# Shift gradient's rounds five job pieces sooner, and the last row block of w1's gradient summed in two column halves

## The chip, the core and the metric

The kernel runs on one core of one Trainium2 chip. The metric is the device time of one execution in microseconds (us). Before the change it is 702.48 us, the median of 3 runs (701.94 to 702.93).

A core has engines that work side by side, each with its own instruction queue, executed in order: TensorE (PE, matrix products; its weight loads are shown apart as PEld), VectorE (DVE), ScalarE (ACT), GpSimd (POOL) and SyncE (SP). SP, ACT and POOL also issue DMA transfers, each from its own queue. Engines wait for one another with semaphores. Matrix products are written to PSUM, a small memory of banks, and ACT or DVE copy them from there.

## The reference

The reference runs a four-layer model forwards, and then computes the gradients of its output with respect to eight inputs. S = 2048 rows, D = 448 columns, F = 1792 hidden columns, all in bf16.

```
x = A_q
x = x + A(layernorm(x), k, v, shift_k, ssm_k, ssm_D)   # A: k_shift = 4-tap causal shift of k weighted by shift_k
x = x + B(layernorm(x), w1, w2)                         #    kv = k_shift * v
x = x + A(layernorm(x), ...)                            #    y  = causal convolution of kv with ssm_k over S (FFT) + kv * ssm_D
x = x + B(layernorm(x), w1, w2)                         #    A  = q * y          (q is the normed x)
return x                                                # B: silu(x @ w1) @ w2
outputs: x, and the gradients for A_q, k, v, shift_k, ssm_k, ssm_D, w1, w2
```

Two of the outputs matter here. Output 7 is the gradient of w1, a 448 x 1792 matrix: the sum, over both B layers, of (normed input of the layer)ᵀ times (gradient at the hidden layer). Output 4 is the gradient of shift_k, a 448 x 4 matrix: for each of the 448 channels and each of the four taps, the sum over all 2048 rows of k, shifted, times the gradient of k_shift.

## The kernel before, in words

The kernel has a prefix (FFT of the convolution's kernel and of kv), a main part (the four layers forwards and backwards, in four chunks of 512 rows) and a suffix (`_ssm_suffix`: the gradients that go backwards through the FFT, and those of k, v, shift_k, ssm_k and ssm_D).

**Job pieces.** The weight gradients of w1 and w2 are long sums that need nothing but operands which the main part has stored in DRAM. The class `Jobs` holds them as a generator (`steps`): each step, a *piece*, puts four matmuls on PE. The suffix calls `jobs.run(n)` between its own steps, and each such call puts n pieces into PE's instruction order at that place. `jobs.run(1000)` on the last line of the suffix takes what is left. PE's order is exactly this written order (`manual_schedule`); the instructions of the other engines are put in order by the framework's scheduler.

**One row block of w1's gradient.** The gradient is computed transposed, in 14 row blocks of 128 of the 1792 hidden columns. For a block, `group` loads two stationary operands from DRAM (`dstat`, 128 x 2048 each, one for each layer, on SP's queue), and `mms` sums 2 x 16 matmuls into one PSUM bank (`ps_d`, 128 x 448, line L1046): 16 with the moving operand `n3m`, 16 with `n1m`. These are eight pieces. `fin_w1` then copies the sum with ACT to SBUF (`dout`, L1120), and `flush` does the rest for the block *before*: four transposes on PE (`ps_dt`, L1133), a copy to `wts` (L116 on ACT), and a DMA to output 7 (L1136). That block's flush so lies behind the sum of the block after it. For blocks 0 to 11 the DMA is issued by POOL, for block 12 by SP and for block 13 by ACT; block 13's copy to `wts` is on DVE (L117). Banks for `ps_d` are taken in turn by `bank(None)` from the tags "po", "tr" and "po", each of two buffers.

**The shift gradient.** After the last products of the ssm_k gradient (`ps_gK`, L1300), the suffix computes the shift gradient in four *rounds* r (`ps_sk`, L1322, two buffers of the tag "mm"): 64 small matmuls on 32 x 32 blocks of the array (32 in the last round), whose diagonals DVE reads out with a mask (`skjunk`, L1325). Before round 0 stands `jobs.run(8)`, after each round `jobs.run(3)`. Then DVE casts the result (`gskb`, L1329 and L1331), three further pairs of rows of the k gradient (`g_k`) are written on DVE and POOL, `jobs.run(3)` follows, and four matmuls with the identity turn the result (`ps_r`, L1337, in a buffer of the tag "po"). ACT copies it (`gsr`, L1339), and two DMAs store it, one on SP (L1341) and one on POOL (L1342). Last stands `jobs.run(1000)`.

With these numbers of pieces, the pieces of the last block end in the `jobs.run(3)` behind round 2, and `jobs.run(1000)` issues no matmul any more. L1370 is the closing code at the end of the program: each queue waits for its transfers and drains, then all engines meet.

Of the kernel before, what the change touches and what calls it, by code (L numbers as in the profile page):

```python
# [17 lines left out]
P = 128  # L18
S = 2048
D = 448  # L20
F = 1792
J = 16
NT = 16
DC = 112
ND = 4
# [88 lines left out]
def _copy(nc, eng, out, in_):  # L114
    if eng is nc.scalar:
        return nc.scalar.copy(out, in_)  # L116
    return eng.tensor_copy(out, in_)  # L117
# [18 lines left out]
def kernel(  # L136
# [63 lines left out]
    with tc.manual_schedule(engines={nc.tensor.engine}):  # L200
        with ExitStack() as es:
            Main(k, es).run(ys)
        _ssm_suffix(k)
# [369 lines left out]
class Main:  # L573
# [142 lines left out]
    def first_norm(self, xc, n00, n01):  # L716
        prs = ((0, 2), (2, 4))
        steps = [_ln_parts(self.k, self.ch, 0, self.xs(0), 1, n01, (pr,), True) for pr in prs]
        for pr, step in zip(prs, steps):
            self.gate(0, lambda tl: xc[:, tl, :], n00, (pr,), self.tc.keep_in_program_order)  # L720
            if pr[0]:
                next(steps[0], None)
            next(step)
        next(steps[1], None)
# [277 lines left out]
class Jobs:  # L1002
# [37 lines left out]
            nc.sync.dma_start_transpose(out=st, in_=src[ft, :, :])  # L1040
        return st

    def mms(self, ps, st, mov, lo, hi, first, last):
        for t0 in range(lo, hi, 4):
            for t in range(t0, t0 + 4):
                self.nc.tensor.matmul(ps[:, :D], lhsT=st[:, t, :], rhs=mov[:, t, :], start=(first and t == 0), stop=(last and t == NT - 1))  # L1046
            yield 1

    def bank(self, tag):
        if tag is None:  # L1050
            tag = ("po", "tr", "po")[self.n_bank % 3]
            self.n_bank += 1
        bufs = 2
        if tag == "mm":
            return self.k.psum.tile([P, 2, 512], FP32, name="ps_d", tag="mm", bufs=2)[:, 0, :]
        return self.k.psum.tile([P, 512], FP32, name="ps_d", tag=tag, bufs=bufs)[:]
# [25 lines left out]
    def steps(self):  # L1082
        g2 = lambda: self.k.mov2
        go = lambda: self.go
        keys = (("a", 1), ("a", 0))
        yield from self.group((0, 1, 2), keys, (go, g2), self.fin_w2, 12, ("tr", "po", "mm"))
        for f in range(3, 12):
            yield from self.group((f,), keys, (go, g2), self.fin_w2, tags=("tr",) if f == 3 else None)
        yield from self.group((12, 13), keys, (go, g2), self.fin_w2)
        keys = (("g", 1), ("g", 0))  # L1090
        movs = (lambda: self.n3, self.n1)
        yield from self.group((0, 1, 2), keys, movs, self.fin_w1)
        for f in range(3, 14):
            yield from self.group((f,), keys, movs, self.fin_w1)
        self.flush()

    def n1(self):
# [20 lines left out]
    def fin_w1(self, ft, ps):  # L1118
        o = self.out()
        self.nc.scalar.copy(o[:], ps[:, :D])  # L1120
        self.flush()
        self.pend = (ft, o)

    def flush(self):
        nc, k = self.nc, self.k
        if self.pend is None:
            return
        ft, o = self.pend
        self.pend = None
        out7v = k.outs[7].rearrange("(c p) f -> p c f", p=DC)  # L1130
        pt = k.psum.tile([DC, ND, P], BF16, name="ps_dt", tag="tr", bufs=2)
        for dc in range(ND):
            nc.tensor.transpose(pt[:, dc, :], o[:, dc * DC:(dc + 1) * DC], k.ident[:])  # L1133
        o7 = k.do7[ft % 4]
        _copy(nc, nc.vector if ft == 13 else nc.scalar, o7, pt[:])
        (nc.scalar if ft == 13 else nc.sync if ft == 12 else nc.gpsimd).dma_start(out=out7v[:, :, ft * P:(ft + 1) * P], in_=o7)  # L1136


def _s1_gy(k, rows):
# [6 lines left out]
def _ssm_suffix(k):  # L1146
    nc, tc, bal = k.nc, k.tc, k.bal
    jobs = k.jobs
# [6 lines left out]
    with ExitStack() as es:  # L1155
# [29 lines left out]
        for g in range(7):  # L1185
            pt = psum.tile([P, 2, 16, 64], BF16, name="ps_tr", **mm)
# [78 lines left out]
        for i in range(8):  # L1265
# [7 lines left out]
            last = nc.scalar.copy(gkv, py[:, :, :D])  # L1273
# [34 lines left out]
        gDr = sp.tile([ND, DC], BF16, name="gDr")  # L1308
        nc.scalar.copy(gDr[:], pr[:ND, :DC])
        nc.gpsimd.dma_start(out=k.outs[6].rearrange("(c p) -> c p", p=DC), in_=gDr[:])  # L1310
        jobs.run(8)
        mask = sp.tile([P, 32], BF16, name="mask")
        for q in range(4):
            nc.vector.tensor_copy(mask[32 * q:32 * q + 32, :], k.ident[32 * q:32 * q + 32, 32 * q:32 * q + 32])
# [60 lines left out]
```

## Time and profile before

| | before |
|---|---|
| median of the runs | 702.48 us (701.94 to 702.93) |
| profiled execution, its own time | 701.8 us |
| span of the profiled execution | 700.0 us |
| granted TensorE clock | 0.998 of full speed |
| DMA traffic over the span | 66.05 MB read, 54.60 MB written |

The profile comes from one execution. Its span runs from the first to the last instruction; the time of the execution is 1.8 us longer. Lines of the timeline read: start in us from the span's beginning, length in us, engine, line of the kernel, operation, what is written `<-` what is read, shapes, and xN where N instructions were merged; in brackets stands how long the engine had been idle and who released it. A "q" behind an engine's name is its queue, which issues DMAs and waits. The length of a merged run of matmuls holds the latency of its last one, so the pace of a run is read from two runs of different lengths, or from the start of one to the start of the next. The lines of the closing code give the count of instructions, their shortest, median and longest duration in ns, and the first and the last start. For DMAs the profile gives the size and the time from issue to landing.

### The profile page before, as it was taken

The page shows a single profiled execution, that of the slowest core. Times are in us where ns is not written, and L with a number is a line of the kernel's source. Part 1 is how long each engine was busy: PE and PEld are TensorE (multiplying, and loading weights), DVE is VectorE, ACT ScalarE, POOL GpSimd, SP SyncE. Part 2 cuts the span into 40 slices and gives each one's busy share as a digit, 9 for nine tenths or more (in the row PEclk, how much of TensorE's full clock was granted, in tenths as well). Part 3 has the DMA queues.
Part 4 walks back from the last instruction along what each step waited for, and adds up shares of the span by engine and source line. Part 5 has one row for each costly group of instructions (what it writes and reads, how often), then busy time and mean ns, then how long its engine had stood idle before and what let it go on. Part 6 is the DMA issues. An engine that isn't in the chain of part 4 may idle for free.

```text
span 700.0 us, 14553 instructions
## 1 busy us (share of the span) xinstructions
PE 666.0 (95%) x5897; PEld 358.8 (51%) x5933; DVE 484.1 (69%) x1131; ACT 432.9 (62%) x522; POOL 101.3 (14%) x173
## 2 busy tenths in 40 slices
PE   6898789999999999999999999999999999999996
PEld 5876545454444444434444444544554555555664
DVE  6688862676889948899578874853946545538991
ACT  5888766968856857769577585223554553554431
POOL 1057110110011100111000100010111211102311
PEclk9999999999999999999999999999999999999999
DMA  8999938459899976698677799959557888966981
GB/s 321 270 298 306 376 84 210 118 107 243 219 231 249 246 200 166 146 240 221 185 165 194 194 242 329 262 172 229 177 208 280 307 279 307 352 188 215 331 293 42
DMA packets 199798, 161.03 MB, mean 230 GB/s; under 512 B 147698, under 2 KB 180213, under 8 KB 198963
## 3 DMA queue, kind: packets, MB, share of 16 engines
q1 hardware_dynamic: 184550, 111.78, 58.8%
q0 software_dynamic: 10368, 36.29, 15.3%
q10 hardware_dynamic: 4812, 12.04, 5.0%
q8 instruction: 46, 0.75, 0.4%
q14 instruction: 22, 0.17, 0.1%
HBM read 66.05 MB, written 54.60 MB: 172 GB/s over the span
## 4 chain that ended last, share of the span: by engine, by line
PE 57%; DVE 22%; issue 10%; ACT 5%; POOL 3%; DMA 2%; POOLq 0%; DVEq 0%; ACTq 0%
PE ps_d L1046 19%; PE ps_n L836 8%; PE ps_h L638 6%; PE ps_g L638 6%; PE ps_o L798 5%; DVE ln_st L301 2%; DVE lb_v L994 2%; PE ps_v L265 2%; PE ps_cv L449 2%; POOL rstd L306 2%; DVE n L309 1%; DVE lb_v L997 1%; DVE lb_v L998 1%; DVE X L802 1%; PE ps_h L642 1%
## 5 line engine op out<-in xcount | busy, mean ns | idle before, releaser
L1046 PEld LDWEIGHTS <-dstat 128*128 128x128 bf16 x896 | 84.0, 98 | 77.8 <-issue 4.0
L836 PE MATMUL ps_n<-w1T,ghT 128*128 128x448 bf16 x448 | 96.6, 353 | 2.0 <-DVE ghT L821 1.7
L798 PE MATMUL ps_o<-w2sb,aT 128*128 128x448 bf16 x448 | 89.2, 353 | 0.7 <-DVE X L802 0.7
L638 PE MATMUL ps_h<-nT,w1sb 128*128 128x512 bf16 (+1 forms) x410 | 83.5, 336 | 2.2 <-ACT Dall L116 1.0
L116 ACT CAST ghT<-ps_g 128x1024 bf16<-128x1024 f32 (+1 forms) x54 | 48.4, 899 | 58.4 <-PE ps_g L642 47.7
L638 PE MATMUL ps_g<-nT,w2T 128*128 128x512 bf16 x317 | 77.9, 379 | 2.2 <-DVE Dall L117 0.5
L836 PEld LDWEIGHTS <-ghT 128*128 128x128 bf16 x448 | 41.4, 98 | 50.7 <-DVE ghT L821 6.7
L798 PEld LDWEIGHTS <-aT 128*128 128x128 bf16 x448 | 43.2, 98 | 41.1 <-issue 2.8
L638 PEld LDWEIGHTS <-w1sb 128*128 128x128 bf16 x420 | 39.2, 98 | 36.7 <-issue 7.2
L781 ACT ACTIVATE aT<-ps_h 128x1024 bf16<-128x1024 f32 (+1 forms) x48 | 44.2, 921 | 19.4 <-PE ps_h L638 10.5
L116 ACT CAST Dall<-ps_h 128x1024 bf16<-128x1024 f32 (+2 forms) x60 | 54.3, 904 | 0.0
L994 DVE SCALAR_TENSOR_TENSOR lb_v<-lb_u,n 128x448 bf16<-128x448 bf16 x60 | 37.2, 620 | 24.6 <-ACT lb_u L840 24.1
L791 ACT ACTIVATE Dall<-Dall 128x1024 bf16<-128x1024 bf16 (+1 forms) x48 | 53.2, 1186 | 0.1
L638 PEld LDWEIGHTS <-w2T 128*128 128x128 bf16 x336 | 31.3, 98 | 42.1 <-issue 7.2
L306 POOL TENSOR_TENSOR rstd<-ln_ve,mhalf 128x2 f32<-128x2 f32 (+1 forms) x24 | 19.9, 831 | 221.1 <-DVE ln_ve L305 221.1
L1046 PE MATMUL ps_d<-X,dstat 128*128 128x448 bf16 x224 | 47.9, 353 | 0.0
L1046 PE MATMUL ps_d<-go,dstat 128*128 128x448 bf16 x224 | 47.2, 353 | 0.0
L1046 PE MATMUL ps_d<-n3m,dstat 128*128 128x448 bf16 x224 | 46.4, 353 | 0.0
L1046 PE MATMUL ps_d<-n1m,dstat 128*128 128x448 bf16 x224 | 46.3, 353 | 0.0
L840 ACT ACTIVATE lb_u<-ps_n,rstd 128x448 bf16<-128x448 f32 x32 | 20.5, 640 | 28.7 <-PE ps_n L836 24.3
L116 ACT CAST A1g<-ps_v 128x1024 bf16<-128x1024 f32 x14 | 14.9, 1066 | 36.5 <-PE ps_v L265 36.5
L802 DVE TENSOR_TENSOR X<-X,ps_o 128x448 bf16<-128x448 bf16 x32 | 19.5, 610 | 21.3 <-PE ps_o L798 21.1
(206 smaller groups left out, 1111.6 us busy)
## 6 DMA issues: line engine op xcount, KB each, us to landing
dstat<-a_d SPq DMA_DIRECT2D x28, 512.0 KB, 5.0
dstat<-g_d SPq DMA_DIRECT2D x28, 512.0 KB, 5.2
a_d<-turned SPq DMA_DIRECT2D x16, 512.0 KB, 3.0
g_d<-turned SPq DMA_DIRECT2D x16, 512.0 KB, 3.2
a_d<-turned SPq DMA_DIRECT2D x16, 384.0 KB, 2.7
g_d<-turned SPq DMA_DIRECT2D x16, 384.0 KB, 3.0
spec_K<-KAB POOLq DMA_DIRECT2D x7, 512.0 KB, 5.4
KAB<-KAB POOLq DMA_DIRECT2D x28, 128.0 KB, 4.6
```

The lines of the kernel that those rows point to most:

```text
L116: return nc.scalar.copy(out, in_)
L265: nc.tensor.matmul(pv[:, r ^ (ci & 1), i, :], lhsT=src[ri, i * P:(i + 1) * P], rhs=k.Gsb[ri, g, ri], start=first, stop=not first)
L306: nc.gpsimd.tensor_tensor(out=r[:, lo:hi], in0=ve[:, lo:hi], in1=k.mhalf[:, lo:hi], op=ALU.pow)
L638: self.nc.tensor.matmul(ps, lhsT=w[:, b, ft * P:(ft + 1) * P], rhs=x[:, b], start=(start and b == 0), stop=(stop and b == bs[2]))
L781: self.last_silu = nc.scalar.activation(aT[hh][:, o:o + hi - lo, :], ps(lo, hi), ACT.Silu)
L791: self.nc.scalar.activation(dT[hh][:, o:o + n, :], dT[hh][:, o:o + n, :], ACT.Derivative_silu)
L798: nc.tensor.matmul(po[:, :D], lhsT=aT[ft // 7][:, ft % 7, tl * P:(tl + 1) * P], rhs=self.w2sb[:, ft, :], start=(ft == 0), stop=(ft == NF - 1))
L802: self.last_o = nc.vector.tensor_tensor(out=X[:, t, :], in0=X[:, t, :], in1=po[:, :D], op=ALU.add)
L836: nc.tensor.matmul(pn[:, :D], lhsT=gh[ft // 7][:, ft % 7, tl * P:(tl + 1) * P], rhs=self.w1T[:, ft, :], start=(ft == 0), stop=(ft == NF - 1))
L840: nc.scalar.activation(u0[:], pn[:, :D], ACT.Identity, scale=k.rstd[2 * L + 1][:, t:t + 1], accum_out=cp[:, tl, 0:1])
L994: nc.vector.scalar_tensor_tensor(out=v[:], in0=u0, scalar=-1.0 / D, in1=n_t, op0=ALU.mult, op1=ALU.mult, accum_out=cp[:, 1:2])
L1046: self.nc.tensor.matmul(ps[:, :D], lhsT=st[:, t, :], rhs=mov[:, t, :], start=(first and t == 0), stop=(last and t == NT - 1))
```

## The change

First, `jobs.run(8)` before the shift gradient's rounds becomes `jobs.run(3)`. Five pieces (20 matmuls) that stood before round 0 come behind it, and everything after it in PE's order moves with respect to the pieces.

Second, block 13 of w1's gradient is no longer made by `group` but by a new function, `last`. It loads both stationary operands and sums the two halves of 224 columns one after the other, each in a bank of its own and with all 32 stationary operands: 64 matmuls of 224 columns in place of 32 of 448. ACT copies each half (two copies of 224 columns). `flush` takes the range of transposes that it is to do: block 12 is flushed in half 0 behind its seventh piece, half 0 in half 1 behind its third piece, half 1 at the end.

Third, block 13's two stores are issued by SP (two halves, each behind a DVE copy of 256 columns), and block 12's store by POOL.

In PE's order of the changed kernel, the first rounds stand behind 8 matmuls of block 12 (n3m), 12 more, and 12 more; the fourth stands behind the first 12 narrow matmuls of block 13. `ps_r` stands behind the first 4 narrow matmuls of half 1, and waits for ACT, whose copy of half 0 frees its bank. Behind it follow 8 narrow matmuls, two transposes of half 0, 20 narrow matmuls, and two transposes of half 1. SP's last transfers are the shift gradient's and then the two halves' stores; POOL's last are the stores of blocks 10, 11 and 12 and the shift gradient's. DVE's order is the same but for the copies of `ps_dt` at its end. Lines behind L1048 are 17 or 18 higher in the changed kernel (L1133 is L1151, L1337 is L1355, L1370 is L1388); ACT's copy of a half is L1061.

```diff
-    def mms(self, ps, st, mov, lo, hi, first, last):
+    def mms(self, ps, st, mov, lo, hi, first, last, cols=slice(0, D)):
         for t0 in range(lo, hi, 4):
             for t in range(t0, t0 + 4):
-                self.nc.tensor.matmul(ps[:, :D], lhsT=st[:, t, :], rhs=mov[:, t, :], start=(first and t == 0), stop=(last and t == NT - 1))
+                self.nc.tensor.matmul(ps[:, cols], lhsT=st[:, t, :], rhs=mov[:, t, cols], start=(first and t == 0), stop=(last and t == NT - 1))
             yield 1
+
+    def last(self, ft, keys, movs):
+        nc, k = self.nc, self.k
+        sts = [self.load(key, ft) for key in keys]
+        o = self.out()
+        for h in range(2):
+            cols = slice(h * D // 2, (h + 1) * D // 2)
+            ps = self.bank(None)
+            for i in range(2):
+                for n, _ in enumerate(self.mms(ps, sts[i], movs[i](), 0, NT, i == 0, i == 1, cols)):
+                    if h + i == 1 and n == 2:
+                        self.flush()
+                    yield 1
+            nc.scalar.copy(o[:, cols], ps[:, cols])
+            if h == 0:
+                self.flush()
+            self.pend = (ft, o, 2 * h, 2 * h + 2)
...
-        for f in range(3, 14):
+        for f in range(3, 13):
             yield from self.group((f,), keys, movs, self.fin_w1)
+        yield from self.last(13, keys, movs)
         self.flush()
...
-        self.pend = (ft, o)
+        self.pend = (ft, o, 0, ND)
...
-        ft, o = self.pend
+        ft, o, lo, hi = self.pend
...
-        for dc in range(ND):
+        for dc in range(lo, hi):
             nc.tensor.transpose(pt[:, dc, :], o[:, dc * DC:(dc + 1) * DC], k.ident[:])
         o7 = k.do7[ft % 4]
-        _copy(nc, nc.vector if ft == 13 else nc.scalar, o7, pt[:])
-        (nc.scalar if ft == 13 else nc.sync if ft == 12 else nc.gpsimd).dma_start(out=out7v[:, :, ft * P:(ft + 1) * P], in_=o7)
+        _copy(nc, nc.vector if ft == 13 else nc.scalar, o7[:, lo:hi], pt[:, lo:hi])
+        (nc.sync if ft == 13 else nc.gpsimd).dma_start(out=out7v[:, lo:hi, ft * P:(ft + 1) * P], in_=o7[:, lo:hi])
...
         nc.gpsimd.dma_start(out=k.outs[6].rearrange("(c p) -> c p", p=DC), in_=gDr[:])
-        jobs.run(8)
+        jobs.run(3)
         mask = sp.tile([P, 32], BF16, name="mask")
```

## The prediction

> **What bounds the kernel now.** I read the page's busy rows first, then the end of the chain of waits, then the timeline of the last 25 us, and last the closing instructions.
>
> ```profile
> PE 666.0 (95%) x5897; PEld 358.8 (51%) x5933; DVE 484.1 (69%) x1131; ACT 432.9 (62%) x522; POOL 101.3 (14%) x173
> ```
> ```profile
> 686.23 9.93 issue
> 696.15 0.54 POOLq L1370
> ```
>
> TensorE (PE) is busy 95% of the span, so any matmul time added or any hole in its stream shows. The chain, however, ends not on PE but on POOL, which idles 9.93 us and then issues the last transfer. The timeline shows what POOL waited for:
>
> ```profile
> 690.22 2.44 PE L1046 MATMUL ps_d<-n1m,dstat 128*128 128x448 bf16 x12
> 692.59 1.07 PE L1322 MATMUL ps_sk<-kx_s,gks 128*32 128x128 bf16 x32
> 693.59 0.65 PE L1133 MATMUL ps_dt<-ident,dout 128*112 128x128 bf16 x8
> 694.06 0.59 ACT L116 COPY wts<-ps_dt 112x512 bf16<-112x512 bf16 x1 [0.83 <-PE ps_dt L1133]
> 694.34 0.42 DVE L117 COPY wts<-ps_dt 112x512 bf16<-112x512 bf16 x1
> 694.67 0.34 SPq L1136 DMA_DIRECT2D out_dram<-wts  x1
> 694.68 0.15 DVE L1331 CAST gskb<-gsk 64x4 bf16<-64x4 f32 x1
> 694.89 0.39 PE L1337 MATMUL ps_r<-ident,gskb 128*4 128x128 bf16 x4 [0.64 <-DVE gskb L1331]
> 695.31 0.57 ACT L1339 CAST gsr<-ps_r 4x512 bf16<-4x512 f32 x1 [0.66 <-PE ps_r L1337]
> 695.91 0.32 SPq L1341 DMA_DIRECT2D out_dram<-gsr  x1
> 696.17 0.52 POOL L1342 DMA_DIRECT2D out_dram<-gsr  x1 [9.95 <-ACT gsr L1339]
> ```
>
> PE has no hole to 694.2. The last shift-gradient round (ps_sk, 692.59) is followed by DVE's gskb, PE's ps_r and ACT's gsr; only then do SP (695.91) and POOL (696.17) issue the shift gradient's two stores. Two queues then close:
>
> ```profile
> L1370 SPq EVENT_SEMAPHORE  x2: 28/28/28, 697.3 to 697.9; - x2
> L1370 SPq DRAIN  x2: 7/7/7, 698.3 to 698.4; - x2
> L1370 POOLq DRAIN  x1: 3064/3064/3064, 696.2 to 696.2; - x1
> L1370 PEldq EVENT_SEMAPHORE  x1: 51/51/51, 700.0 to 700.0; - x1
> out_dram<-wts SPq DMA_DIRECT2D x1, 112.0 KB, 2.3
> SPq L1370 <- DMA out_dram<-gsr: 0.6, 1, 0.6
> ```
>
> SP sees its last store land at 697.9 (695.91 + 2.0) and is drained at 698.4. POOL's drain starts at 696.15 with its last issue and takes 3.06 us, to 699.2; 0.8 us of common closing follow. So POOL sets the end, 0.8 us after SP would.
>
> **The change part by part.** Quoted once, the steps of PE that both versions share, and the widths that the halves need:
>
> ```profile
> 676.83 3.19 PE L1046 MATMUL ps_d<-n3m,dstat 128*128 128x448 bf16 x16
> 682.22 1.08 PE L1322 MATMUL ps_sk<-kx_s,gks 128*32 128x128 bf16 x64
> 683.23 0.93 PE L1046 MATMUL ps_d<-n1m,dstat 128*128 128x448 bf16 x4
> 684.00 0.39 PE L1133 MATMUL ps_dt<-ident,dout 128*112 128x128 bf16 x4
> 684.22 1.68 PE L1046 MATMUL ps_d<-n3m,dstat 128*128 128x448 bf16 x8
> 685.83 1.08 PE L1322 MATMUL ps_sk<-kx_s,gks 128*32 128x128 bf16 x64
> 686.84 1.69 PE L1046 MATMUL ps_d<-n3m,dstat 128*128 128x448 bf16 x8
> 689.21 1.08 PE L1322 MATMUL ps_sk<-kx_s,gks 128*32 128x128 bf16 x64
> 30.49 0.94 PE L465 MATMUL ps_s<-ks_kv,M1sb 128*128 128x224 bf16 x8
> L465 PE MATMUL ps_s<-ks_kv,M1sb x64: 256/259/270, 30.5 to 52.4; 128*128 128x224 bf16 x64
> ```
>
> *Rounds five pieces sooner.* A piece is four matmuls; 20 of them move behind round 0. At (1.68 − 0.93)/4 = 0.19 us each (runs of 8 and of 4) that is 3.8 us: round 0 starts at 678.44 (676.83 + 1.61, the step from 684.22 to 685.83) instead of 682.22. Are its operands there? kx is, and DVE reads a round's result late:
>
> ```profile
> 652.02 1.41 ACTq L1285 DMA_DIRECT2D kx_s<-in_A_k_dram  x2
> DMA to landing us min/median/max: 13.7/13.9/14.2
> 681.29 1.09 DVE L1261 TENSOR_TENSOR gk<-wx 128x896 bf16<-128x896 f32 x1
> 683.35 0.19 DVE L1325 SCALAR_TENSOR_TENSOR skjunk<-ps_sk,mask 128x32 bf16<-128x32 f32 x1 [0.97 <-PE ps_sk L1322]
> ```
>
> kx landed by 667. DVE keeps its order, so round 0's four readings (at most 4 × 0.19 us) wait for gk, to 682.4, and are done by 683.2. The two banks of ps_sk make round 2 wait for that; it starts at 685.2. The cover is 2.0 us, and DVE's order puts nothing else before it; were it gone, PE would stand for what gk is later than that. Cost: nothing.
>
> *The halves.* 64 matmuls of 224 columns replace 32 of 448. L465 has this very form: (0.94 − 0.26)/7 = 0.097 us each, so 6.21 us for 32 × 0.19 = 6.08, **+0.13 us**. ACT gains one copy; block 12's store goes from SP to POOL (0.7 us of POOL, before it waits for gsr, so nobody waits for it).
>
> *PE's new schedule*, the generated order with the steps above: round 0 678.44 to 679.45; 12 matmuls (686.84 to 689.21 = 2.37), round 1 681.82 to 682.83; 12 (690.22 to 692.59 = 2.37), round 2 685.20 to 686.21; four transposes 0.22, to 686.43; 12 narrow 1.16 and 0.10 for the turn to a round (2.37 − 12 × 0.19, rounded), round 3 687.69 to 688.69 (692.59 to 693.59 = 1.00); 16 narrow 1.55, to 690.24; block 12's four transposes, 690.46; the last 4 narrow of half 0 and the first 4 of half 1, 691.24.
>
> *A new wait.* ps_r, next on PE, needs the bank that half 0 held, so it waits for ACT's copy of half 0. ACT comes to that late: its store copy of block 12 waits for the transposes (690.24 + 0.39), runs from 690.67, and the next ACT instruction starts 0.47 behind it (670.30 to 670.77 below), 691.14. A copy of 224 columns takes 0.53 less half the column cost, (1.01 − 0.53)/576 × 224 = 0.19, so 0.35: done 691.49, ps_r at 691.55. PE stands **0.31 us** in order; everything left of half 1 is queued behind it. Bounds: 0 (if ACT's start is 0.3 earlier) and 0.6 (copy at the full width's 0.53, and a delay of ACT of 0.1).
>
> ```profile
> 670.30 0.59 ACT L116 COPY wts<-ps_dt 112x512 bf16<-112x512 bf16 x1
> 670.77 0.21 ACT L1304 COPY gKD<-gK 112x1 bf16<-112x1 bf16 x1
> 672.02 1.01 ACT L1301 CAST gK<-ps_gK 112x1024 bf16<-112x1024 f32 x1 [1.04 <-PE ps_gK L1300]
> 692.70 0.53 ACT L1120 CAST dout<-ps_d 128x448 bf16<-128x448 f32 x1 [7.48 <-PE ps_d L1046]
> ```
>
> *The new tail.* ps_r 0.22, to 691.77; gsr on ACT and both its stores follow by 692.7, so POOL's drain ends near 692.9 + 3.0 = 695.9 and bounds nothing. PE goes on: 8 narrow 0.78, 2 transposes of half 0 0.11, 20 narrow 1.94, to 694.60; the last one's result 0.16 later, 694.76. ACT 0.04 + 0.35, 695.15. PE 0.05 + 0.28 (the four's 0.39 less two steps), 695.48. DVE 0.04 + 0.30 (half the columns of 0.42, whose ends are 0.21 and 0.42), 695.82. SP issues at **695.84**, just where its last store went before (695.91).
>
> Landing: the 3 KB gsr took 2.0 us, a whole block's store 2.3; half a block 2.15, between. So 697.99 (before 697.9). SP's remaining semaphores and drain took 697.9 to 698.4; 0.45 gives 698.44, bounds 0.1 (its semaphore is the last asked for) and 0.5. Closing as before, 0.8: the span ends at **699.24 for 700.0, −0.76 us**. The gain is POOL's late drain, nothing more: PE's stream gets longer, and the SP queue's last issue stays. The profiled execution took 701.8 (1.8 outside the span), the median is 702.48; I take the difference off the median: **701.7**.
>
> **A rule weighed.** The Trainium skill, "TensorE: Matmul & The Clock Gate", section on LDWEIGHTS, prices a weight load at its columns over 1.2, 107 ns for 128. If that paced the narrow matmuls, 64 × 0.010 = 0.64 us would come on top, an estimate from that page, and 702.4. The trace's L465 spacing of 97 ns disagrees with it as a pace.
>
> **The rivals.**
> - *Much of the tail is early* (faster): no stall at ps_r (−0.31), landing in 2.0 (−0.15), SP's semaphore last asked for (−0.35): 0.76 + 0.81 = 1.57, 700.9. For it: each is an end of a bound above. Against: all three are needed, since 1.4 us decides.
> - *POOL's drain follows the last landing, not POOL's own issue* (no gain): it ended 1.1 us behind the last store's landing (696.17 + 1.9 = 698.1). Then 697.99 + 1.1 + 0.8 = 699.9, 702.4. Against: it began with POOL's issue. That would be the change not doing what it says.
> - *Weight loads pace the narrow matmuls* (slower): one load takes 97 ns and half 1 loads all 32 stationaries again. Unhidden, a matmul would cost 0.097 twice, 64 × 0.097 = 6.2 us more, 708; it decides from 0.131 us a matmul (2.16 us more eats the gain and 1.4). Against: the 0.097 spacing holds while a load of 97 ns runs under each.
>
> ```profile
> L465 PEld LDWEIGHTS <-M1sb 128*128 128x128 bf16 x64 | 5.9, 97 | 2.1 <-issue 0.8 <-DVE ks_kv L455 0.3
> DMA to landing us min/median/max: 1.9/1.9/1.9
> ```
>
> **How the numbers follow.** 0.2% is 1.4 us, about what a measurement of this kernel can tell from no change. My forecast (a small gain inside that) 0.50 and the drain rival 0.12 make "same" 0.62; the early tail, with gains that I have not seen, 0.27 faster; the weight-load rival 0.06 and an unseen stall 0.05 slower. Range: down to the early tail's 700.9 with 0.3 for the runs' own scatter (701.94 to 702.93), 700.6; up to the drain rival's 702.4 with 0.5 for it, 702.9.
>
> **What would show it.** Right: four ps_sk groups from about 678.4, 681.8, 685.2 and 687.7; narrow ps_d matmuls 97 ns apart; ps_r near 691.5 with a hole of about 0.3 us before it that ACT's dout ended; SP's last store at 695.8; POOL's 3 us drain over by 696; the span near 699.2. Wrong: a narrow spacing above 0.13 us, a POOL drain that still ends after SP's, or a hole at round 2 or at the last transposes.

## The result and the profile after

The changed kernel takes 701.64 us (median of 19 runs, 700.62 to 702.49), the kernel before, measured beside it, 702.85 (19 runs, 701.82 to 703.62): ratio 0.9978, 95% interval 0.9971 to 0.9984, so 0.22% less (0.16 to 0.29). Run again later (e8 below, 12 runs, with 35 of the kernel before beside them), the ratio was 0.9987, interval 0.9975 to 0.9999. The kernel is faster, by 0.22% in one series and 0.13% in the other; both intervals end below 1. The profiled execution took 700.62, its span is 698.8 for 700.0.

First the page's busy line of the changed kernel, and from its chain of waits the last pieces:

```profile
PE 668.7 (96%) x5965; PEld 361.8 (52%) x5965; DVE 484.2 (69%) x1132; ACT 432.9 (62%) x523; POOL 102.1 (15%) x174
```
```profile
690.68 0.58 ACT wts L116
691.27 0.26 ACT dout L1061
691.52 0.04 issue
691.57 0.38 PE ps_r L1355 x4
691.95 0.87 PE ps_d L1046 x8
692.82 0.11 PE ps_dt L1151 x2
692.93 1.93 PE ps_d L1046 x20
694.87 0.02 issue
694.89 0.35 ACT dout L1061
695.24 0.04 issue
695.29 0.33 PE ps_dt L1151 x2
695.62 0.02 issue
695.64 0.29 DVE wts L117
```

POOL is no longer at the chain's end. The chain now runs through PE, with a bend over two copies of ACT (block 12's and half 0's) to ps_r at 691.57, and ends with half 1's copies. The timeline of the changed kernel gives the rounds, the narrow matmuls and the last stores:

```profile
678.43 1.08 PE L1340 MATMUL ps_sk<-kx_s,gks 128*32 128x128 bf16 x64
...
681.81 1.08 PE L1340 MATMUL ps_sk<-kx_s,gks 128*32 128x128 bf16 x64
...
685.20 1.08 PE L1340 MATMUL ps_sk<-kx_s,gks 128*32 128x128 bf16 x64
...
687.71 1.07 PE L1340 MATMUL ps_sk<-kx_s,gks 128*32 128x128 bf16 x32
688.72 0.56 PE L1046 MATMUL ps_d<-n3m,dstat 128*128 128x224 bf16 x4
689.11 1.31 PE L1046 MATMUL ps_d<-n1m,dstat 128*128 128x224 bf16 x12
...
690.87 0.55 PE L1046 MATMUL ps_d<-n3m,dstat 128*128 128x224 bf16 x4
691.57 0.38 PE L1355 MATMUL ps_r<-ident,gskb 128*4 128x128 bf16 x4 [0.15 <-ACT dout L1061]
691.88 0.94 PE L1046 MATMUL ps_d<-n3m,dstat 128*128 128x224 bf16 x8
```
```profile
692.85 0.53 POOL L1360 DMA_DIRECT2D out_dram<-gsr  x1 [0.58 <-ACT gsr L1357]
695.96 0.32 SPq L1154 DMA_DIRECT2D out_dram<-wts  x1
```

And the closing instructions of the changed kernel, with the landing of SP's last store:

```profile
L1388 POOLq DRAIN  x1: 2828/2828/2828, 692.8 to 692.8; - x1
L1388 SPq EVENT_SEMAPHORE  x6: 28/28/28, 697.6 to 697.9; - x6
L1388 SPq DRAIN  x2: 7/7/7, 698.0 to 698.1; - x2
DMA to landing us min/median/max: 1.7/1.7/1.7
```

The reader is to see three things. The rounds stand at 678.4, 681.8, 685.2 and 687.7. POOL's drain begins at 692.8 and is over at 695.6, where it ended at 699.2 before. And SP, whose last issue stayed in its place (695.96 for 695.91), now ends the kernel: its store lands 1.7 us later, at 697.6, its drain is at 698.1, and 0.8 us of common closing follow.

### The profile page after: what moved, and what is told of

Read it like the earlier page. It is cut to its first block, busy times and chain, and to the rows that moved or that the text cites. A ratio compares the mean times of both kernels' runs of the same rounds, so it can differ in the third digit from the quotient of the medians.

```text
span 698.8 us, 14657 instructions
## 1 busy us (share of the span) xinstructions
PE 668.7 (96%) x5965; PEld 361.8 (52%) x5965; DVE 484.2 (69%) x1132; ACT 432.9 (62%) x523; POOL 102.1 (15%) x174
## 4 chain that ended last, share of the span: by engine, by line
PE 69%; DVE 16%; ACT 6%; issue 5%; DMA 3%; POOL 2%; DVEq 0%; ACTq 0%; POOLq 0%
PE ps_d L1046 25%; PE ps_n L836 9%; PE ps_h L638 7%; PE ps_o L798 6%; PE ps_g L638 6%; DVE ln_st L301 2%; PE ps_v L265 2%; PE ps_cv L449 2%; POOL rstd L306 2%; DVE lb_v L994 2%; PE ps_h L642 2%; DVE X L802 1%; ACT Dall L116 1%; DVE n L309 1%; PE ps_g L642 1%
## 5 line engine op out<-in xcount | busy, mean ns | idle before, releaser
L1046 PEld LDWEIGHTS <-dstat 128*128 128x128 bf16 x928 | 86.8, 98 | 75.3 <-issue 4.0
L638 PE MATMUL ps_g<-nT,w2T 128*128 128x512 bf16 x336 | 79.5, 379 | 1.0 <-DVE Dall L117 0.5
L994 DVE SCALAR_TENSOR_TENSOR lb_v<-lb_u,n 128x448 bf16<-128x448 bf16 x60 | 37.2, 620 | 24.6 <-ACT lb_u L840 24.1
L1046 PE MATMUL ps_d<-n3m,dstat 128*128 128x448 bf16 (+1 forms) x240 | 47.0, 340 | 0.0
L1046 PE MATMUL ps_d<-n1m,dstat 128*128 128x448 bf16 (+1 forms) x240 | 46.5, 340 | 0.0
L840 ACT ACTIVATE lb_u<-ps_n,rstd 128x448 bf16<-128x448 f32 x32 | 20.5, 639 | 28.7 <-PE ps_n L836 24.3
```

Of the source, the lines that this page charges most:

```text
L638: self.nc.tensor.matmul(ps, lhsT=w[:, b, ft * P:(ft + 1) * P], rhs=x[:, b], start=(start and b == 0), stop=(stop and b == bs[2]))
L840: nc.scalar.activation(u0[:], pn[:, :D], ACT.Identity, scale=k.rstd[2 * L + 1][:, t:t + 1], accum_out=cp[:, tl, 0:1])
L994: nc.vector.scalar_tensor_tensor(out=v[:], in0=u0, scalar=-1.0 / D, in1=n_t, op0=ALU.mult, op1=ALU.mult, accum_out=cp[:, 1:2])
L1046: self.nc.tensor.matmul(ps[:, cols], lhsT=st[:, t, :], rhs=mov[:, t, cols], start=(first and t == 0), stop=(last and t == NT - 1))
```

## The experiments

The time from the first instruction to the suffix's end differed between profiled executions by up to 3.5 us, nearly all of it gathered in the first 100 us, where the kernels do nothing different (but for e7's loads of v). So traces are compared from a common mark, the start of the single ps_r matmul of gKD (675.70 in the trace of before, 675.69 in that of the changed kernel), behind which the other differences lie. The place of the mark goes with the granted clock at the start. Where that was 1.00 in every window of the first 100 us (before, changed kernel, e4, e6), the mark lies at 675.7 to 676.1. With one window below (0.96 over 60 to 100 us, in e1, e2, e5 and e7) it lies at 676.7 to 678.2, with two (0.91 over 20 to 40 us and another, in e3 and e8) at 678.4 and 679.2. That the lower clock is the cause is not shown. This scatter is larger than the gain, and arises ahead of all that the change moves. From the mark to the end the kernel before takes 24.3 us, the changed one 23.1. The time from the mark to the end is called the tail. The tails come from one trace each; the ratios come from the runs. Ratios are against the kernel before, run beside it on the same chip: one chip for e1 to e4, another for e5 to e8.

My theory: the end is the later of two, POOL's last issue with its drain, or SP's last landing with its closing; the change takes POOL out and leaves SP. The rivals: the sooner rounds are the gain by themselves; or the shorter tail of block 13 is, and POOL's drain only fills a wait that is there anyway.

**Each part alone, POOL's store alone, and the hole alone.**

*e1: the rounds sooner, block 13 whole.*

```diff
 # kernel before
-        jobs.run(8)
+        jobs.run(3)
         mask = sp.tile([P, 32], BF16, name="mask")
```

> The kernel before with only the five pieces moved behind round 0; block 13 stays whole. My theory (the end is set by POOL's last issue plus its drain of some 3 us, or by SP's last landing, whichever is later): ps_r stands behind the transposes of blocks 12 and 13 in PE's order, so gsr is made only some 0.25 us sooner than before and POOL's store is issued near 695.9; span 699.7, 0.3 us less than before (0 to 0.5). The rival that the earlier rounds themselves are the gain: the span of the changed kernel, 698.8, 1.2 us less than before.

Measured: ratio 1.0003 (0.999 to 1.0016). Its timeline's mark, round 0 and last issues, and its closing:

```profile
678.19 0.21 PE L1307 MATMUL ps_r<-ident,gKD 112*4 112x112 bf16 x1
...
680.93 1.08 PE L1322 MATMUL ps_sk<-kx_s,gks 128*32 128x128 bf16 x64
...
697.90 0.34 ACTq L1136 DMA_DIRECT2D out_dram<-wts  x1
698.30 0.32 SPq L1341 DMA_DIRECT2D out_dram<-gsr  x1
698.57 0.52 POOL L1342 DMA_DIRECT2D out_dram<-gsr  x1 [7.79 <-ACT gsr L1339]
```
```profile
L1370 POOLq DRAIN  x1: 3610/3610/3610, 698.5 to 698.5; - x1
DMA to landing us min/median/max: 2.5/2.5/2.5
```

The rounds are sooner (round 0 starts 2.7 us behind the mark, for 6.5 before), but ps_r still stands behind all of block 13, and POOL issues 20.4 us behind the mark, where it did before (20.5). The rival falls: sooner rounds gain nothing by themselves that runs or trace would show. My 0.3 us did not come either: POOL's store landed in 2.5 us (before 1.9), and the drain was 3.6 us long (3.06), so the tail is 24.7.

*e2: block 13 in halves, the rounds where they were.*

```diff
 # changed kernel
-        jobs.run(3)
+        jobs.run(8)
         mask = sp.tile([P, 32], BF16, name="mask")
```

> The changed kernel with eight pieces ahead of round 0 again; block 13 in two halves. My theory: ps_r now stands 8 narrow matmuls ahead of the end and finds its bank free long before, so the hole of 0.3 us ahead of it goes; POOL's shift-gradient store is issued near 694.6 and its drain is over near 697.5; SP's last store is issued near 695.6 and lands 1.7 us later. Span 698.4, 0.4 us less than the changed kernel and 1.6 less than before. The rival that the five pieces are needed for the gain: POOL is late again, span near 700.0.

Measured: ratio 0.998 (0.9965 to 0.9995), tail 23.0 (mark 676.73, span 699.7). In its timeline ps_r follows the narrow matmuls with no wait in its row. The last rows are the drains of POOL (the longest of three, which starts first) and of SP:

```profile
693.52 0.93 PE L1046 MATMUL ps_d<-n1m,dstat 128*128 128x224 bf16 x8
694.38 0.39 PE L1355 MATMUL ps_r<-ident,gskb 128*4 128x128 bf16 x4
...
695.67 0.52 POOL L1360 DMA_DIRECT2D out_dram<-gsr  x1 [3.49 <-ACT gsr L1357]
...
696.75 0.34 SPq L1154 DMA_DIRECT2D out_dram<-wts  x1
```
```profile
L1388 POOLq DRAIN  x3: 46/103/2827, 695.6 to 699.5; - x3
L1388 SPq DRAIN  x3: 7/7/7, 698.9 to 699.2; - x3
```

POOL issues 18.9 us behind the mark, and is drained at 698.5, before SP. So the halves, with their new queues, give the whole gain without the sooner rounds, since the 64 narrow matmuls come in twice as many pieces: the same `jobs.run` calls take half as much of block 13, and the rest, 8 narrow matmuls, is left behind ps_r. The five pieces are not needed for it. SP's last store goes 20.0 us behind the mark, for 20.3 in the changed kernel, whose ps_r waits for half 0's bank. By its tail e2 is 0.1 us ahead of the changed kernel where I had expected 0.4, as the store landed in 1.8 us for 1.7; the intervals can't tell the two apart.

*e3: the kernel before, POOL's last store on ACT's queue.*

```diff
 # kernel before
-        nc.gpsimd.dma_start(out=out4f[1536:1792]...)
+        nc.scalar.dma_start(out=out4f[1536:1792]...)
```

> The kernel before, whose second store of the shift gradient is issued by ACT in place of POOL; nothing else. My theory: POOL's last issue is then at 685.5 and its drain is over long before; SP's chain sets the end, span 699.2, 0.8 us less than before. The rival that the halved tail of block 13 is the gain and POOL's drain only fills a wait that is there anyway (it ends when the last transfer has landed): no gain, 700.0.

Measured: ratio 0.9983 (0.9967 to 0.9999), tail 23.4. The rows of its mark, its last matmuls and issues, and SP's drain:

```profile
678.44 0.21 PE L1307 MATMUL ps_r<-ident,gKD 112*4 112x112 bf16 x1
...
697.64 0.39 PE L1337 MATMUL ps_r<-ident,gskb 128*4 128x128 bf16 x4 [0.64 <-DVE gskb L1331]
...
698.66 0.32 SPq L1341 DMA_DIRECT2D out_dram<-gsr  x1
698.66 0.24 ACTq L1342 DMA_DIRECT2D out_dram<-gsr  x1
```
```profile
L1370 SPq DRAIN  x3: 7/7/7, 701.0 to 701.3; - x3
```

PE does just what it did before (ps_r 19.2 us behind the mark in both), and the tail is 0.9 us shorter. This single word carries three quarters of the tail's 1.2 us, and the rival that POOL's drain only fills a wait falls.

*e4: the changed kernel, ps_r in a bank of its own.*

```diff
 # changed kernel
-        pr = psum.tile([P, 512], FP32, name="ps_r", tag="po", bufs=2)
+        pr = psum.tile([P, 512], FP32, name="ps_r", **mm)
         for j in range(4):
```

> The changed kernel, whose ps_r takes a buffer of the rounds' tag, free since round 2 was read, and not the one that half 0 holds. My theory: the hole of 0.32 us on PE ahead of ps_r goes and all that follows comes 0.3 us sooner: SP's last store near 695.65, span 698.5, 0.3 less than the changed kernel. If SP's last landing is not what sets the end now, the span stays 698.8 though the hole is gone.

Measured: ratio 0.9971 (0.9955 to 0.9988), tail 22.9 (mark 676.07, span 699.0).

```profile
691.25 0.55 PE L1046 MATMUL ps_d<-n3m,dstat 128*128 128x224 bf16 x4
691.73 0.39 PE L1355 MATMUL ps_r<-ident,gskb 128*4 128x128 bf16 x4
...
696.13 0.32 SPq L1154 DMA_DIRECT2D out_dram<-wts  x1
```

From the four narrow matmuls to ps_r it is 0.48 us here and 0.70 in the changed kernel: the wait for the bank is worth 0.22 us, and SP's last store and the end come as much sooner. I had expected 0.3. This is the shortest tail of e1 to e4, but the interval does not part it from the changed kernel's.

**What the last store and the closing cost.**

*e5: half 1's store on POOL.*

```diff
 # changed kernel
-        (nc.sync if ft == 13 else nc.gpsimd).dma_start(...)
+        (nc.sync if ft == 13 and hi < ND else nc.gpsimd).dma_start(...)
```

> The changed kernel, whose last store (half 1 of block 13) POOL issues in place of SP. Times here run from the last ps_r of gKD (675.7 in both traces), since the runs so far differed by up to 2.7 us ahead of it; the changed kernel ends 23.15 behind it. My theory, with the runs so far: POOL's drain ends 1.1 to 1.25 us behind the landing of POOL's own last store, so 20.3 for the issue, 1.6 to 2.5 for the landing, 1.2 and 0.75: the end at 23.9 to 24.7, 0.7 to 1.5 later though nothing else moved. The rival that POOL's drain is no bound of its own: the end stays at 23.15.

Measured: ratio 0.9996 (0.9986 to 1.0006), tail 24.6. The whole gain is gone. The rows of the store and of the two drains:

```profile
697.62 0.67 POOL L1154 DMA_DIRECT2D out_dram<-wts  x1 [2.85 <-DVE wts L117]
```
```profile
L1388 SPq DRAIN  x2: 7/7/7, 700.0 to 700.0; - x2
L1388 POOLq DRAIN  x1: 3284/3284/3284, 697.6 to 697.6; - x1
DMA to landing us min/median/max: 2.1/2.1/2.1
```

SP is drained at 700.0, POOL at 700.9. So not all of the 1.5 us that the tail is longer than the changed kernel's is POOL's drain: SP, which is drained only after this landing, is already some 0.5 us later than there, since POOL issues the store 0.3 us later and it lands in 2.1 us for 1.7. POOL's drain adds the other 0.9. The length of POOL's drain less the landing of POOL's last store is 1.2 here (3.28 and 2.1), 1.2 before (3.06 and 1.9), 1.1 in e1 (3.61 and 2.5), 1.2 in the changed kernel (2.83 and 1.6).

*e6: block 13 stored at once.*

```diff
 # changed kernel, in flush
+        if hi < ND:
+            return
-        (nc.sync if ft == 13 else nc.gpsimd).dma_start(out=out7v[:, lo:hi, ...], in_=o7[:, lo:hi])
+        (nc.sync if ft == 13 else nc.gpsimd).dma_start(out=out7v[:, :, ...], in_=o7)
```

> The changed kernel, whose half 0 keeps its copies but is not stored by itself: one store of the whole block 13 on SP at the end (448 runs of 256 bytes in place of 224). It tells what made the last store land in 1.66 us where I took 2.15. If the size: it lands in 2.0 to 2.3 and the end moves to 23.5 to 23.8 behind the mark. If it was the other store in flight beside it (before: SP's and ACT's stores of blocks 12 and 13 at once): 1.7 to 1.8, the end at 23.2 to 23.3.

Measured: ratio 0.9987 (0.9973 to 1.0001), tail 23.7 (mark 676.00, span 699.7). The store of the whole block goes out alone, and still takes 2.1 us to land:

```profile
696.28 0.35 SPq L1156 DMA_DIRECT2D out_dram<-wts  x1
DMA to landing us min/median/max: 2.1/2.1/2.1
```

So it is the size: 112 KB land in 2.1 us alone (2.3 beside another before), 56 KB in 1.7. The trace shows this; the ratio is that of e8, the changed kernel itself. With its last store whole, the changed kernel's tail (23.7) is longer than that of e3 (23.4), which has none of the change: by these traces, what it gains beyond e3 hangs on the halved store. Moving block 13's store from ACT to SP, without halving it, was not tried by itself.

*e7: the last store on the last semaphore.*

```diff
 # kernel of e4, in the prefix
-        for h in range(2):
-            nc.sync.dma_start(out=vn[:, 8 * h:8 * h + 8, :], in_=v_pm[:, 8 * h:8 * h + 8, :])
+        for lo, hi in ((0, 2), (2, 4), (4, 6), (6, 8), (8, 11), (11, 14), (14, 16)):
+            nc.sync.dma_start(out=vn[:, lo:hi, :], in_=v_pm[:, lo:hi, :])
```

> The kernel of e4 (ps_r in its own bank), with the prefix's load of v in seven pieces rather than two, so that the last store falls on the last of the eight transfer semaphores, which SP asks for in order. My theory: behind the last landing SP asks for none more, where it asked for five, 0.06 us each, so its drain follows the landing by 0.1 and not 0.4: the end 0.3 us sooner than e4, 22.6 behind the mark. If the closing takes its 0.4 us whatever the order: 22.9 as in e4.

Measured: ratio 0.9982 (0.9968 to 0.9996), tail 22.8 (mark 676.73, span 699.5). From SP's closing, in two stretches:

```profile
L1388 SPq EVENT_SEMAPHORE  x8: 27/28/28, 697.1 to 697.6; - x8
```
```profile
L1388 SPq DRAIN  x2: 7/7/7, 698.7 to 698.8; - x2
L1388 SPq EVENT_SEMAPHORE  x1: 28/28/28, 698.6 to 698.6; - x1
DMA to landing us min/median/max: 1.8/1.8/1.8
```

Eight semaphores are asked for ahead of the landing and one behind it; in the changed kernel six are asked for behind it (697.6 to 697.9). SP's first drain follows the landing by 0.1 us and not 0.4. The end came only 0.1 us sooner than in e4, as the store landed in 1.8 us for e4's 1.6.

*e8: the changed kernel again.*

> The changed kernel once more, for comparison on the same chip: the end 23.15 behind the mark, and 0.1 to 0.3% less than the kernel before.

Measured: ratio 0.9987 (0.9975 to 0.9999), tail 23.3 (mark 679.23, span 702.5). Its last store landed in 1.8 us, which is the 0.15 us to the first trace; the same half store took 1.6 to 1.8 us over the traces.

## Why the prediction was right, point by point

- *POOL sets the end, 0.8 us after SP would*: right, and shown by e3 (tail 0.9 shorter with PE untouched) and e5 (the gain lost when POOL issues last again).
- *Rounds cost nothing, round 2 covered*: right. The four rounds stand within 0.03 us of the forecast places, and none waits.
- *Narrow matmuls, 0.097 us each*: right; (1.31 − 0.56)/8 = 0.094 in the changed kernel. The weight-load rival falls. The 107 ns of the rule weighed (128 columns over 1.2, an estimate by the Trainium skill's page "TensorE: Matmul & The Clock Gate", section on LDWEIGHTS) is not the pace here.
- *The new wait at ps_r*: right in place and cause. Forecast 691.55, measured 691.57; but only 0.22 us of the 0.31 are the bank's, and 0.09 stay when ps_r has a bank of its own (e4).
- *SP's last issue in its old place*: 695.84 forecast, 695.96 measured, 695.91 before. Of the 0.12 us more, 0.02 lie ahead of ps_r, and 0.09 are ps_r itself: the next matmul starts 0.31 behind it (691.57 to 691.88), where the sum has 0.22.
- *The failed step: "half a block 2.15, between".* The bounds, 2.0 for 3 KB and 2.3 for a whole block, both belong to stores that were in flight together. The half store went out with nothing else in flight and landed in 1.7, outside them, so the span came out at 698.8 for 699.24, and the tail fell by 1.2 for 0.76. By e6's trace half the size is worth some 0.45 us when nothing else is in flight (0.3 to 0.5, as the half store took 1.6 to 1.8). That SP's gsr took 2.0 because two whole stores lay ahead of it is argued, not shown. POOL's 512 bytes landed in 1.9 and 2.5 us with two whole stores in flight (before, e1), and in 1.6 with one ahead of them (changed kernel) or none (e2).
- *The early tail, 700.9*: of the three ends of bounds that it needed, only the landing came, and went beyond its 2.0; the wait at ps_r and the 0.45 behind the landing stayed.
- *0.45 from the landing to SP's drain*: right (697.6 to 698.1), with the cause that I had put at a bound: SP asks for the semaphores in turn, and in e7, where the store's semaphore is the last, the drain followed by 0.1.
- *The drain rival* was wrong in saying that it follows the last landing of any queue: in the changed kernel it ended at 695.6, 2 us before SP's last landing. But my own form, that it takes some 3 us from POOL's issue, was not right either: it ends 1.1 to 1.2 us behind the landing of POOL's own last store, in four traces.
- *The median, 701.7*: 701.64. It fell so near by luck: the gain was 1.21 us for the 0.76 forecast, and the median of before over all 19 runs lies 0.37 us above the 702.48 that I subtracted from. By its ratio the gain, 0.22%, lies just beyond the 0.2% that I drew between same and faster; by the later series' 0.13%, and by the tail's 1.2 us (0.17%), it lies inside, which I held likelier.

That the sooner rounds serve the gain, as the change is put together, isn't borne out: with the halves, eight pieces ahead of round 0 do as well (e2), and without the halves, three pieces ahead do nothing (e1).

## What to carry to other kernels

At the end of a kernel, write out for each queue its last issue, its landing and its closing; the latest of these sums is the end, whatever the share of PE. A store of a few hundred bytes on POOL's queue, issued last, cost 0.9 us here, and naming another queue took it away. A last output cut in two lets the first part's copies and store run under the second's matmuls and halves what must land at the end, but look which bank the next small product will take: half 0's bank made PE wait.

## What I had not expected of the hardware

- POOL's closing drain ended 1.1 to 1.2 us behind the landing of its last store (drains of 2.83, 3.06, 3.28 and 3.61 us for landings of 1.6, 1.9, 2.1 and 2.5, in the changed kernel, before, e5 and e1).
- SP asks for its transfers' semaphores one after another at the end, 0.06 us each; where the last store's semaphore stands in that order is worth 0.3 us (e7: first drain 0.1 us behind the landing, for 0.4).
- The same store of 56 KB landed in 1.6 to 1.8 us from execution to execution, as much as some of the changes tried here are worth.
